# A long convolution beside attention on one core: two channels per matmul, filter rows in quarters

## The chip, the core and the metric

The kernel runs on one core of a Trainium2 chip. The metric is the device time of one execution in microseconds. Five engines work side by side: TensorE (PE, matmuls; PEld are its weight loads), VectorE (DVE), ScalarE (ACT), GpSimd (POOL) and SyncE (SP), which here only issues DMAs.

## The reference

Two independent blocks are computed and put side by side in the output (2048 x 1024, bf16).

- A: multi-head attention with S = 2048, D = 512 and 32 heads of 16: `qkv = x @ wqkv`, `p = softmax(q k^T / 4)`, `o = p v`, `out = o @ wo`.
- B: a gated long convolution of 512 channels. `k_shift` is `k` filtered along time with four taps per channel, `kv = k_shift * v`, then

```
y[t, c] = sum over u <= t of kv[u, c] * ssm_k[c, t - u]     (written as an FFT of length 4096)
y = y + kv * ssm_D
out = q * y
```

So for each channel B is a product with a lower triangular Toeplitz matrix of 2048 x 2048.

## The kernel before

**Attention.** Scores are made in blocks of 128 keys x 512 queries for one head; there are 2048 of them. A matmul (L728) puts a block in one of six PSUM banks. ScalarE takes the exp of two or three banks with one instruction (L761) into the ring PT. Part of the blocks, one in a step where VectorE has time, is done on VectorE with four operations: a scaling to fixed point (L803), two squaring steps (L810 twice) and a last step (L815), into the ring PTD. The PV matmuls (L844) accumulate in bank PVB. `finish_group` turns and normalises the result; `op_mm` multiplies with `wo`.

**Steps and the planner.** The program is written out ahead of time by a planner in Python. It keeps a modelled time for each engine (`pe.t`, `dve.t`, `done`), and in a loop over steps T it emits the score matmuls and the exp of step T, the PV of step T - 2, background work and filler matmuls (`emit_qk`, `pv_step`, `emit_bg`, `warm_up`). Each engine then runs its list in order, with semaphore waits. The planner's constants are PACE, RATE, CAP, LAGS (how many convolution lags a step may take), MARGIN, TURN, NEAR and HALF (by how much a background unit may overrun), PLAN (the step by which the work is spread), and FETCH (after how many us a block of 256 instructions of TensorE is counted as loaded; `Tensor.spare` holds work back near that point). Up to step N_OPEN the background units of the list `early` run, in bank BGB or PVB; after it those of `jobs`, for which a bank is taken from the steps for a few steps (a window, `win`, `hold`). A VectorE operation that frees a bank is placed at once (`urgent`); the rest of VectorE's work is put into the gaps (`advance`).

**The convolution.** The taps of `k_shift` are diagonal matrices (DG); `pe_unit` makes `k_shift` of 128 channels and 512 times in a bank, and `evac_unit` multiplies it with v into KV (L511 to L514). The filter, reversed in time and padded, is written to DRAM once (`kz_scratch`, from KZS). `load_wr` reads for each channel a [128, 2048] tile of it in which partition p starts one element after partition p - 1 (L996): 512 KB per channel, four channels (one `qd`) per slot of WR, four slots, the last of which is free only when the v tiles that it holds at first are used up. `conv_lags` makes for a `qd` 16 lags of 128 times, each as four matmuls, one per channel, in four groups of 32 columns of the array: the weights are KV (128 times x up to 16 blocks), the moving operand 128 columns of WR. Lag n pairs each block with the block n before it. Out come 16 of each 32 partitions of bank BGB. After four `qd` VectorE copies the bank to YB (L1028), and after eight `conv_turn` makes eight transposes of YB on TensorE and one multiplication with q (L1048). WR's DMAs all go through SP's queue, and a slot's reload is issued when the slot's last lag is done.

Of the kernel before, what the change touches and what calls it, by code (L numbers as in the profile page):

```python
# [9 lines left out]
U16 = mybir.dt.uint16  # L10

S = 2048
# [11 lines left out]
C = 512  # L24
NB = S // 128
PAD = 128
# [3 lines left out]
R_W = 16  # L30
# [6 lines left out]
N_OPEN = 66  # L37
# [26 lines left out]
CLOSE = 12  # L64
# [7 lines left out]
PLAN = 710  # L72
# [3 lines left out]
Q_DUE = 24  # L76
# [9 lines left out]
DMA_KB = 394  # L86
X_KB = 200
WINDOW = 3.4
HALF = 0.25
TURN = 0.2  # L90
SOON = 0.5
NEAR = 0.2
FULL = 1.6
BUSY = 0.85
FILL_GAP = 0.2
RATE = 4.2
CAP = 14.0
WAIT = 1.5
LATE = 0.2
# [8 lines left out]
FETCH = 6.3  # L108
# [111 lines left out]
def bass_concat_heads__mha_block__ssm_conv_h3__prompt_kernel(  # L220
# [36 lines left out]
    KV = sb("KV", [128, C // 4, NB, 4])  # L257
# [143 lines left out]
    h_va1 = pool.op(lambda e: e.memset(VA[:, :, :, 8 * VW:VROW].rearrange("p s k e -> p (s k) e"), 1.0))  # L401
    h_qt0 = pool.op(lambda e: e.memset(QT[:, 1:R_Q, :, :].rearrange("p r n f -> p (r n f)"), 0.0), us=(1.5, 1.6))
# [87 lines left out]
    def evac_unit(u, bank, h):  # L490
        kind = u[0]
        if kind == "q":
            p = u[1]
            last = [qk_done[2 * (p - R_Q) + i] for i in range(2)] if p >= R_Q else []
            hh = urgent(lambda e: e.tensor_scalar(QS[:, :], PS[:, bank, :], QSCALE, None, ALU.mult),
                        [h] + [h_q[2 * (p - 1) + i] if p > 1 else None for i in range(2)], us=V512)
            for par in range(2):
                for r0 in range(16 * par, 128, 32):
                    h_q[2 * p + par] = dma(pool, d_qs[p % 2][par], QT[r0:r0 + 16, p % R_Q, par, :], QS[r0:r0 + 16, :],
                                           [hh, h_qt0] + last, kb=16)  # L500
        elif kind == "k":
            _, o, sc = u
            c0 = KEYS0 if (o, sc) == (0, 0) else 0
            hh = urgent(lambda e: e.tensor_copy(KTo[:, o % 2, sc * 512 + c0:(sc + 1) * 512], PS[:, bank, c0:512]),
                        [h, qk_done[LAST[o - 2]] if o > 1 else None], us=(0.335, 0.46) if c0 else V512)
            h_k[(o, sc)] = hh
            if (o, sc) == (3, 3):
                load_wop(h)
        elif kind == "kv":
            _, c, i = u  # L510
            dst = KV[:, 32 * c:32 * c + 32, NB - 4 - 4 * i:NB - 4 * i, :]  # L511
            val = VST[c][:, NB - 4 - 4 * i:NB - 4 * i, :].rearrange("p b (k c) -> p k b c", c=4)
            src = PS[:, bank, :].rearrange("p (b k c) -> p k b c", b=4, c=4)
            h_kvc[c] = hh = urgent(lambda e: e.tensor_tensor(dst, src, val, ALU.mult), [h, h_vn[c]], us=V512)  # L514
            kv_n[c] += 1
            if sum(kv_n[0:2]) == 8 and c < 2:
                load_qn(0, [h])
                wr_free.append((R_W // 4 - 1, hh))
                load_wr()
            if c >= 2 and kv_n[c] == 4:  # L520
                h_kvm[c - 2] = h
        else:
            _, o, sc = u
            dst = VA[:, o % 2, 4 * sc:4 * sc + 4, 0:8 * VW].rearrange("p k (h e) -> p k h e", e=VW)[:, :, :, 0:DH]
            src = PS[:, bank, :].rearrange("p (k h e) -> p k h e", k=4, h=8)
            hh = urgent(lambda e: e.tensor_copy(dst, src), [h, h_va1, pv_last[LAST[o - 2]] if o > 1 else None], us=V512)
            h_v[(o, sc)] = hh
        bank_free[bank] = hh
# [456 lines left out]
    h_yb = [None]  # L985
# [4 lines left out]
    def load_wr():  # L990
        while wr_free and wr_next[0] < C // 4:
            (i, dep), qd = wr_free.pop(0), wr_next[0]
            wr_next[0] += 1
            wr_slot[qd] = i
            for c in range(4):
                src = bass.AP(tensor=kz_ap.tensor, offset=kz_ap[4 * qd + c, 0].offset, ap=[[1, 128], [1, S]])  # L996
                h_wr[qd] = dma(sp, d_wr[i], WR[:, 4 * i + c, :], src, [h_kzw[0], dep])
# [4 lines left out]

    def conv_lags(qd, n0, n1):
        kk = qd % 8
        deps = [h_wr[qd], h_kvc[qd // 32]]
        r = 4 * wr_slot[qd]
        if kk % 4 == 0 and n0 == 0:
            deps.append(bank_free[BGB])

        def fn(e):  # L1010
            ins = None
            for n in range(n0, n1):
                for c in range(4):
                    ins = e.matmul(PS[32 * c:32 * c + NB - n, BGB, 128 * (kk % 4):128 * (kk % 4) + 128],  # L1014
                                   lhsT=KV[:, qd, n:NB, c],
                                   rhs=WR[:, r + c, 128 * (NB - 1 - n):128 * (NB - n)],
                                   start=(n == 0), stop=(n == NB - 1), tile_position=(0, 32 * c))
            return ins
        h = pe.op(fn, deps, run=LAG * (n1 - n0), kind="C", lat=0.4)
        if n1 == NB:  # L1020
            wr_free.append((wr_slot[qd], h))
            load_wr()
            if kk % 4 == 3:
                half = kk // 4
                src = PS[:, BGB, :]
                src = bass.AP(tensor=src.tensor, offset=PS[:, BGB, 127:128].offset,
                              ap=[src.ap[0], [128, 4], [-1, 128]])
                hh = urgent(lambda e: e.tensor_copy(YB[:, half, :].rearrange("p (k i) -> p k i", k=4), src),  # L1028
                            [h, h_yb[0]], slack=S_C, us=V512)
                bank_free[BGB] = h_ybw[0] = hh  # L1030
        return h

    def conv_turn(b, bank):
        pbf = PS[:, bank, :].bitcast(BF16)

        def fn(e):
            ins = None
            for k in range(8):
                ins = e.transpose(pbf[:, 128 * k:128 * k + 128], YB[:, k // 4, 128 * (k % 4):128 * (k % 4) + 128],
                                  IDN[:, :])  # L1040
            return ins
        h = pe.op(fn, [bank_free[bank], h_ybw[0], h_idn], run=0.445, kind="F")
        h_yb[0] = h
        sl = b // 8
        yv = pbf.rearrange("p (c j) -> p c j", j=32)[:, :, 0:NB].rearrange("p c j -> p j c")
        yv = bass.AP(tensor=yv.tensor, offset=pbf[:, NB - 1:NB].offset, ap=[yv.ap[0], [-1, NB], [32, CHB]])
        qv = QN[:, :, CHB * (b % 8):CHB * (b % 8) + CHB]
        hh = urgent(lambda e: e.tensor_tensor(qv, yv, qv, ALU.mult), [h, h_qn[sl]], slack=S_C, us=V512)  # L1048
        bank_free[bank] = hh
        if b % 8 == 7:  # L1050
            dst = out2[:, D + 256 * sl:D + 256 * (sl + 1)].rearrange("(t p) c -> p t c", p=128)
            ho = dma(pool, d_outB[0], dst, QN[:, :, :], [hh], kb=1600)
            if sl == 0:
                load_qn(1, [ho])
# [4 lines left out]
    units = [("kv", c, i) for c in range(2) for i in range(4)] + [(x, 1, i) for i in range(4) for x in "kv"]  # L1059
# [7 lines left out]
    jobs += [(step(9 + 7 * c) - 8, ("kv", c + 2, i)) for c in range(2) for i in range(4)]  # L1067
    jobs += [(step(25 + 2 * qb) + 8 * t, ("op", qb, t)) for qb in range(NQB - 1) for t in range(4)]
    jobs.sort(key=lambda j: j[0])
    state = {"qd": 0, "lag": 0, "turn": False, "started": False, "lags": 0.0, "left": C // 4 * NB, "t": 0.0}  # L1070
# [6 lines left out]
    def next_unit(T):  # L1077
        if T < N_OPEN:
            return early[0] if early and ready(early[0][1]) else None
        if state["turn"]:  # L1080
            return T, ("turn", state["qd"] // 8 - 1)
        return next((j for j in jobs if ready(j[1])), None)
# [5 lines left out]
    def unit_step(T):  # L1088
# [7 lines left out]
        while not tight:  # L1096
# [23 lines left out]
            us = pe.turn("F") + (0.445 if u[0] == "turn" else 0.478 if u[0] in ("kv", "v") else 2 * MM) + SWITCH  # L1120
# [22 lines left out]
    def emit_bg(T):  # L1143
# [5 lines left out]
        if T - end[0] in tail_mm:  # L1149
            assert st["qd"] == C // 4 and not st["turn"], (T, st)  # L1150
# [3 lines left out]
        if st["qd"] == C // 4 and not st["turn"]:  # L1154
# [3 lines left out]
        if st["turn"] and st["qd"] == C // 4:  # L1158
# [11 lines left out]
        while left > 0 and st["qd"] < wr_next[0] and kv_n[st["qd"] // 32] == 4 and at(h_wr[st["qd"]]) + WAIT <= pe.t:  # L1170
            if st["turn"] and st["qd"] % 4 == 3 and st["lag"] + left >= NB:
                left = NB - 1 - st["lag"]
                if left <= 0:
                    break
# [3 lines left out]
            n1 = min(n0 + left, NB)  # L1178
# [4 lines left out]
            st["lag"] = n1 % NB  # L1183
            if n1 == NB:
                st["qd"] += 1
                if st["qd"] % 4 == 0:
                    st["turn"] = st["turn"] or st["qd"] % 8 == 0
                    break

    def filler_place(limit):  # L1190
# [5 lines left out]
        if state["started"] and state["lag"]:  # L1196
            return BGB, 0, NB, 128 * (state["qd"] % 4), 1, False
# [53 lines left out]
    assert state["qd"] == C // 4 and not state["turn"] and not jobs and not part[0], (state, jobs)  # L1251
# [65 lines left out]
```

## Time and profile before

| | |
|---|---|
| three runs | 825.12, 829.2, 827.42 us; median 827.42 us |
| the profiled execution | 828.52 us, of which the span from first to last instruction is 826.8 us |
| ScalarE, VectorE, TensorE busy | 807.0, 794.2, 762.2 us |
| DMA | 291.41 MB, 109,235 packets; q1 (SP's queue) busy for 90.8% |
| exp instructions on ScalarE (L761) | 722, for 1771 blocks |
| blocks on VectorE (L803) | 277 |
| WR<-kz_scratch | 512 DMAs of 512 KB, median 8.4 us from issue to landing |

The busy times of an engine come from its instructions as the profiler saw them, so instructions that overlap are counted once. In a group's line stand the line of the kernel, engine, operation, output <- input with shapes, the count, then the busy time and the mean length of one, then the idle time of the engine before them and what ended it. "issue" is time in which an engine waited for nothing that the profile shows. A DMA share above 1.00 in a short stretch comes from packets that overlap.

### The profile page before, as it was taken

The numbers are of one execution on the slowest core, as the hardware profiler recorded it, in microseconds if no ns is written. First come the engines' busy times: TensorE is split into PE (matmuls) and PEld (weight loads), VectorE is DVE, ScalarE is ACT, GpSimd is POOL, SyncE is SP. The second block draws the span as 40 slices with busy tenths as digits, with TensorE's granted clock in tenths as the row PEclk, the third lists the DMA queues.
The fourth block names the chain that finished last, engine by engine and source line by source line (L and its number), as shares of the span: only waits on it lengthen the run. The fifth ranks groups of instructions, "written<-read, shape, count | busy, mean of one in ns | idle before, by whom it ended". The sixth has DMA issues, their size and how long they took to land.

```text
span 826.8 us, 30549 instructions
## 1 busy us (share of the span) xinstructions
PE 762.2 (92%) x13603; PEld 324.2 (39%) x13642; DVE 794.2 (96%) x1360; ACT 807.0 (98%) x727; POOL 78.7 (10%) x155
## 2 busy tenths in 40 slices
PE   8998989999999899999899999999999999998987
PEld 3343434443333344444333344444433333333332
DVE  4999999999999899999999999999999999999985
ACT  6999999999999899999999999999999999999987
POOL 3300320010100101001011010101002002010000
PEclk9999999999999999999999999999999999999999
DMA  9998499999999999999999899999999999999922
GB/s 220 233 300 304 151 382 404 385 379 407 393 407 405 394 401 389 405 354 367 394 388 391 318 372 383 394 408 387 408 407 352 378 393 362 399 382 367 375 83 77
DMA packets 109235, 291.41 MB, mean 352 GB/s; under 512 B 37680, under 2 KB 41648, under 8 KB 108720
## 3 DMA queue, kind: packets, MB, share of 16 engines
q1 hardware_dynamic: 102256, 280.80, 90.8%
q0 software_dynamic: 5648, 8.27, 3.1%
q8 instruction: 108, 1.77, 0.9%
q10 hardware_dynamic: 1200, 0.39, 0.2%
q14 instruction: 23, 0.19, 0.1%
HBM read 276.83 MB, written 6.42 MB: 343 GB/s over the span
## 4 chain that ended last, share of the span: by engine, by line
ACT 77%; DVE 10%; PE 9%; issue 2%; DMA 1%; SPq 0%
ACT PT L761 77%; DVE EH L810 4%; PE PS L728 3%; DVE FX L803 2%; PE PS L1014 2%; PE PS L844 2%; DVE PTD L815 2%; PE PS L1219 1%; PE PS L468 1%; DMA xT<-in_A_x_dram 1%; DVE DT L905 0%; DVE YB L1028 0%; SPq L312 0%; DVE KV L514 0%; DVE OTN L925 0%
## 5 line engine op out<-in xcount | busy, mean ns | idle before, releaser
L761 ACT ACTIVATE PT<-PS 128x1024 bf16<-128x1024 f32 (+2 forms) x722 | 804.1, 1376 | 8.8 <-PE PS L728 8.3
L728 PE MATMUL PS<-QT,KTo 32*128 32x512 bf16 x2048 | 287.1, 385 | 38.7 <-ACT PT L761 14.1
L844 PE MATMUL PS<-PT,VA 128*32 128x512 bf16 x1771 | 199.7, 391 | 6.6 <-issue 3.5
L1014 PE MATMUL PS<-WR,KV 128*12 128x128 bf16 (+15 forms) x8192 | 201.6, 220 | 4.4 <-issue 4.3
L803 DVE TENSOR_SCALAR FX<-PS 128x512 f32<-128x512 f32 x277 | 187.9, 682 | 8.3 <-PE PS L728 8.0
L815 DVE SCALAR_TENSOR_TENSOR PTD<-EH,FX 128x512 uint16<-128x512 f32 x277 | 185.7, 677 | 0.0
L810 DVE SCALAR_TENSOR_TENSOR EH<-EH 128x512 f32<-128x512 f32 x277 | 185.4, 680 | 0.0
L810 DVE SCALAR_TENSOR_TENSOR EH<-FX 128x512 f32<-128x512 uint16 x277 | 184.5, 682 | 0.1
L1014 PEld LDWEIGHTS PS<-WR,KV 128*12 128x12 bf16 (+15 forms) x8192 | 140.6, 88 | 71.9 <-issue 42.5
L728 PEld LDWEIGHTS PS<-QT,KTo 32*128 32x128 bf16 x2048 | 73.3, 91 | 237.8 <-ACT PT L761 178.9
L1219 PE MATMUL PS<-IDN,ZW 128*32 128x512 bf16 (+3 forms) x498 | 132.2, 334 | 0.0
L312 POOL DMA_DIRECT2D QT<-QS x120 | 59.2, 501 | 483.7 <-DVE DR L912 133.7
L844 PEld LDWEIGHTS PS<-PT,VA 128*32 128x32 bf16 x1771 | 48.0, 93 | 114.0 <-issue 97.5
L844 PE MATMUL PS<-PTD,VA 128*32 128x512 bf16 x277 | 83.1, 383 | 0.0
L1219 PEld LDWEIGHTS PS<-IDN,ZW 128*32 128x32 bf16 x498 | 41.8, 96 | 24.1 <-issue 10.4
L905 DVE STREAM_TRANSPOSE DT<-PS 128x512 f32<-128x512 f32 x32 | 22.7, 709 | 7.3 <-PE PS L844 6.8
L1028 DVE CAST YB<-PS 128x512 bf16<-128x512 f32 x32 | 21.9, 684 | 1.4 <-PE PS L1219 1.1
L844 PEld LDWEIGHTS PS<-PTD,VA 128*32 128x32 bf16 x277 | 20.4, 95 | 1.6 <-DVE PTD L815 0.2
L955 PE MATMUL PS<-WKV,OTN 128*128 128x512 bf16 x53 | 16.9, 383 | 2.1 <-issue 1.6
L479 PE MATMUL PS<-WKV,xT 128*128 128x128 bf16 x256 | 18.1, 220 | 0.1
L456 PE MATMUL PS<-xT,WKV 128*128 128x512 bf16 (+1 forms) x52 | 15.0, 373 | 2.9 <-issue 1.1
L447 PE MATMUL PS<-xT,WQ 128*128 128x512 bf16 x45 | 14.4, 382 | 2.4 <-issue 2.1
(65 smaller groups left out, 209.2 us busy)
## 6 DMA issues: line engine op xcount, KB each, us to landing
WR<-kz_scratch SPq DMA_DIRECT2D x512, 512.0 KB, 8.4
kz_scratch<-WR SPq DMA_DIRECT2D x1, 2176.0 KB, 8.3
QN<-in_B_q_dram POOLq DMA_DIRECT2D x2, 1024.0 KB, 12.4
out_dram<-QN POOLq DMA_DIRECT2D x2, 1024.0 KB, 8.6
QT<-QS POOLq DMA_DIRECT2D x120, 16.0 KB, 5.3
out_dram<-OUTA POOLq DMA_DIRECT2D x12, 128.0 KB, 5.2
QN<-in_B_ssm_k_dram SPq DMA_DIRECT2D x1, 1024.0 KB, 8.3
OTN<-in_B_ssm_k_dram SPq DMA_DIRECT2D x1, 1024.0 KB, 9.2
```

The source lines that it names most:

```text
L312: f(outp, inp).then_inc(dsem.sem, 16)
L479: ins = e.matmul(PS[:, bank, 128 * j:128 * j + 128], lhsT=xT[:, dc, (4 * sc + j) * 128:(4 * sc + j + 1) * 128], rhs=WV[:, dc, o * 128:(o + ...
L728: ins = e.matmul(PS[:, bank, :], lhsT=KTo[32 * s:32 * s + 32, OF[n_] % 2, kt * 128:(kt + 1) * 128], rhs=QT[32 * s:32 * s + 32, n_ // 2 % R ...
L761: h_exp[T] = act.op(lambda e: e.activation(PT[:, p0:p0 + n, :].rearrange("p b f -> p (b f)"), PS[:, banks[0]:banks[0] + n, :].rearrange("p ...
L803: h_f = urgent(lambda e: e.tensor_scalar(fx, PS[:, bank, :], FIX_ADD, FIX_HI, ALU.add, ALU.min), [h, h_last.get(i - R_FX)], slack=S_FX)
L810: st["h"] = dve.op(lambda e: e.scalar_tensor_tensor(eh, src, (P1, P2)[j], src, ALU.add, ALU.mult), [st["h"], h_last.get(i - R_EH)], us=us)
L815: lambda e: e.scalar_tensor_tensor(out16, eh, P3, fx, ALU.mult, ALU.add),
L844: ins = e.matmul(dst, lhsT=w, rhs=rhs, start=(k == 0), stop=(k == KT - 1), tile_position=(0, 32 * s))
L905: h_t = urgent(lambda e: e.transpose(out=dt, in_=PS[:, PVB, :]), [h, h_mul.get(n - 1)], slack=S_T, us=(0.63, 0.751))
L1014: ins = e.matmul(PS[32 * c:32 * c + NB - n, BGB, 128 * (kk % 4):128 * (kk % 4) + 128], lhsT=KV[:, qd, n:NB, c], rhs=WR[:, r + c, 128 * (NB ...
L1028: hh = urgent(lambda e: e.tensor_copy(YB[:, half, :].rearrange("p (k i) -> p k i", k=4), src), [h, h_yb[0]], slack=S_C, us=V512)
L1219: pe.op(lambda e, s=s, k=k, rhs=rhs, bank=bank, rows=rows, c0=c0, first=first: e.matmul(PS[32 * s:32 * s + rows, bank, c0:c0 + 128 * k], l ...
```

## The change

A `qd` is now eight channels in place of four. The 128 rows of the array are split between two channels, 64 times each. The channel pair of a group is 64 channels apart.

- WR has 8 rows in place of 16: two slots. A row holds two channels, 64 partitions each, so a `qd` still has four rows. Its filter tile comes in eight DMAs: four quarters of 512 columns, the last columns first, and for each quarter the two halves of 64 partitions in turn, four rows per DMA (256 KB).
- KV is twice as large and mostly zero for the other channel: a column has the values of one channel in its 64 partitions and zeros in the others, which GpSimd writes once at the start. `evac_unit` therefore splits each product into four operations of 64 partitions.
- `conv_lags` makes 32 lags of 64 times for a `qd`, in the order 0, -1, 1, 2, ... 30, again as four matmuls each; the weights have up to 32 columns (two channels x 16 blocks). Out come all 32 partitions of a group.
- A full bank now holds 32 channels, so VectorE copies half as many banks to YB, and a turn follows each of them, with four transposes.
- The kv units of the second 128 channels move from `early` to `jobs`, and constants of the planner are set anew.

```diff
+NLAG = S // 64
-R_W = 16
+R_W = 8
-N_OPEN = 66
+N_OPEN = 64
+KV1 = 2
-CLOSE = 12
+CLOSE = 10
-PLAN = 710
+PLAN = 715
-Q_DUE = 24
+Q_DUE = 28
+HALF_KB = 270
+WR_C = 512
-TURN = 0.2
+TURN = 0.05
-NEAR = 0.2
+NEAR = 0.1
-FILL_GAP = 0.2
+FILL_GAP = 0.25
-CAP = 14.0
+CAP = 18.0
-LATE = 0.2
+LATE = 0.1
-FETCH = 6.3
+FETCH = 4.2
...
-    KV = sb("KV", [128, C // 4, NB, 4])
+    KV = sb("KV", [128, C // 8, 2, 2 * NB, 4])
...
+    h_kv0 = pool.op(lambda e: e.memset(KV[:, :, :, :, :].rearrange("p o r u g -> p (o r u g)").bitcast(U32), 0), us=(8.8, 8.9))
     h_qt0 = pool.op(lambda e: e.memset(QT[:, 1:R_Q, :, :].rearrange("p r n f -> p (r n f)"), 0.0), us=(1.5, 1.6))
...
-            dst = KV[:, 32 * c:32 * c + 32, NB - 4 - 4 * i:NB - 4 * i, :]
-            val = VST[c][:, NB - 4 - 4 * i:NB - 4 * i, :].rearrange("p b (k c) -> p k b c", c=4)
-            src = PS[:, bank, :].rearrange("p (b k c) -> p k b c", b=4, c=4)
-            h_kvc[c] = hh = urgent(lambda e: e.tensor_tensor(dst, src, val, ALU.mult), [h, h_vn[c]], us=V512)
+            q0 = 2 * (NB - 4 - 4 * i)
+            val = VST[c][:, NB - 4 - 4 * i:NB - 4 * i, :].rearrange("p b (h o g) -> p b h o g", h=2, g=4)
+            src = PS[:, bank, :].rearrange("p (b h o g) -> p b h o g", b=4, h=2, g=4)
+            for half in range(2):
+                for ch in range(2):
+                    hs, cs = slice(64 * half, 64 * half + 64), slice(64 * ch, 64 * ch + 64)
+                    dst = KV[cs, 16 * c:16 * c + 16, 1 - half, q0 + ch:q0 + 8:2, :].rearrange("p o q g -> p q o g")
+                    h_kvc[c] = hh = (dve.op if half or ch else urgent)(
+                        lambda e, dst=dst, hs=hs, ch=ch: e.tensor_tensor(dst, src[hs, :, ch], val[hs, :, ch], ALU.mult),
+                        [h, h_vn[c], h_kv0], us=(0.335, 0.46))
...
-            for c in range(4):
-                src = bass.AP(tensor=kz_ap.tensor, offset=kz_ap[4 * qd + c, 0].offset, ap=[[1, 128], [1, S]])
-                h_wr[qd] = dma(sp, d_wr[i], WR[:, 4 * i + c, :], src, [h_kzw[0], dep])
+            for c0 in range(S - WR_C, -1, -WR_C):
+                for ch in range(2):
+                    row = 128 * (qd // 16) + 64 * ch + 4 * (qd % 16)
+                    src = bass.AP(tensor=kz_ap.tensor, offset=kz_ap[row, c0].offset, ap=[[1, 64], [LKZ, 4], [1, WR_C]])
+                    h_wr[qd] = dma(sp, d_wr[i], WR[64 * ch:64 * ch + 64, 4 * i:4 * i + 4, c0:c0 + WR_C], src,
+                                   [h_kzw[0], dep], kb=WR_C // 2, rate=HALF_KB)
...
+    DIST = [0, -1] + list(range(1, NLAG - 1))
...
-                for c in range(4):
-                    ins = e.matmul(PS[32 * c:32 * c + NB - n, BGB, 128 * (kk % 4):128 * (kk % 4) + 128],
-                                   lhsT=KV[:, qd, n:NB, c],
-                                   rhs=WR[:, r + c, 128 * (NB - 1 - n):128 * (NB - n)],
-                                   start=(n == 0), stop=(n == NB - 1), tile_position=(0, 32 * c))
+                d = DIST[n]
+                w = 64 if d < 0 else 128
+                for g in range(4):
+                    kv = KV[:, qd, (1 + d) % 2, (1 + d) // 2 * 2:2 * NB, g]
+                    ins = e.matmul(PS[32 * g:32 * g + 2 * ((30 - d) // 2 + 1), BGB, 128 * kk:128 * kk + w],
+                                   lhsT=kv, rhs=WR[:, r + g, S - 64 * d - 128:S - 64 * d - 128 + w],
+                                   start=(n == 0), stop=(n == NLAG - 1), tile_position=(0, 32 * g))
...
-            for k in range(8):
-                ins = e.transpose(pbf[:, 128 * k:128 * k + 128], YB[:, k // 4, 128 * (k % 4):128 * (k % 4) + 128],
-                                  IDN[:, :])
+            for k in range(4):
+                ins = e.transpose(pbf[:, 128 * k:128 * k + 128], YB[:, b % 2, 128 * k:128 * k + 128], IDN[:, :])
...
-    units = [("kv", c, i) for c in range(2) for i in range(4)] + [(x, 1, i) for i in range(4) for x in "kv"]
+    units = [("kv", 0, i) for i in range(4)] + [(x, 1, i) for i in range(4) for x in "kv"]
...
+    jobs += [(N_OPEN + KV1 + 4 * i, ("kv", 1, i)) for i in range(4)]
...
-                    st["turn"] = st["turn"] or st["qd"] % 8 == 0
+                    st["turn"] = True
```

## The prediction

> **What bounds the kernel now.** I read the page from the busy shares to the DMA queues and the chain, then the groups of instructions with their shapes kept apart, then the busy time by stretch, and last the timeline around the stretches where ScalarE lost time. First the page: busy shares, then two DMA queues, then the chain that ended last.
>
> ```profile
> PE 762.2 (92%) x13603; PEld 324.2 (39%) x13642; DVE 794.2 (96%) x1360; ACT 807.0 (98%) x727; POOL 78.7 (10%) x155
> q1 hardware_dynamic: 102256, 280.80, 90.8%
> q8 instruction: 108, 1.77, 0.9%
> ACT 77%; DVE 10%; PE 9%; issue 2%; DMA 1%; SPq 0%
> ```
>
> ScalarE is busy for 98% of the span and 77% of the chain is its exp; VectorE stands at 96%; the DMA engines at 91%. All three look full, but only the first sets the end: ScalarE has 1771 of the 2048 score blocks, VectorE 277. The groups (line, engine, shape, count, busy us, mean ns):
>
> ```profile
> L761 ACT ACTIVATE PT<-PS 128x1536 bf16<-128x1536 f32 x321 | 493.9, 1605 | 6.5 <-PE PS L728 6.0
> L761 ACT ACTIVATE PT<-PS 128x1024 bf16<-128x1024 f32 x398 | 429.0, 1188 | 1.0 <-PE PS L728 1.0
> L1028 DVE CAST YB<-PS 128x512 bf16<-128x512 f32 x32 | 21.9, 684 | 1.4 <-PE PS L1219 1.1 <-PE PS L1014 0.2
> L916 DVE TENSOR_TENSOR DTN<-DT,DR 128x256 bf16<-128x256 f32 x32 | 13.3, 415 | 0.0
> ```
>
> The means overlap their neighbours. Taken from start to next start, the usual step is 1.330 us for three blocks and 0.903 us for two, so one block costs ScalarE 0.427 us and one more instruction 0.05 us. On VectorE a 512-column operation takes 0.600 us and a 256-column one 0.332 us in the same way, so a block there costs 4 x 0.600 = 2.4 us. With 321, 398 and 3 instructions (of three, two and four blocks) the floor of ScalarE's exp is 792 us; the trace has 804 busy, so about 12 us are short waits inside the busy time.
>
> Now the stretches (length, then busy time of PE, PEld, DVE, ACT, POOL, clock, DMA share, GB/s):
>
> ```profile
> 80.00:100.00 20.00, 19.29 (x291) 7.54 (x290) 20.00 (x36) 20.00 (x20) 3.83 (x8) 1.00 0.33 99
> 240.00:320.00 80.00, 74.22 (x1455) 31.85 (x1459) 77.52 (x135) 77.93 (x71) 5.78 (x13) 0.98 1.03 400
> 480.00:560.00 80.00, 75.15 (x1484) 33.22 (x1475) 79.60 (x137) 80.00 (x74) 4.65 (x9) 1.00 1.02 396
> 784.00:788.00 4.00, 3.08 (x67) 1.11 (x55) 4.00 (x8) 4.00 (x5) 0.00 (x0) 1.00 1.03 405
> ```
>
> From 400 to 780 us ScalarE loses 0.1 us, with the DMA engines full. What it loses lies elsewhere, in six places, and they look alike. The last, from the timeline:
>
> ```profile
> 786.86 0.40 PE L844 MATMUL PS<-PT,VA 128*32 128x512 bf16 x3
> 789.23 0.40 PE L844 MATMUL PS<-PT,VA 128*32 128x512 bf16 x3 [1.98 <-issue]
> 790.87 2.85 ACT L761 ACTIVATE PT<-PS 128x1536 bf16<-128x1536 f32 x2 [2.13 <-PE PS L728]
> ```
>
> TensorE stops with nothing to wait for, and ScalarE runs dry behind it. In the packet records a 16 KB packet of the instruction queue ends 1.3 to 1.6 us before TensorE resumes, at all six (106.1, 223.8, 230.0, 279.9, 356.0, 789.2 us): TensorE waits for its own code. ScalarE loses 0.42 + 0.46 + 0.62 + 2.00 + 0.58 + 2.13 = 6.2 us there (at 280 and 788 the granted clock drops too), VectorE 7.9 us.
>
> **The change, part by part.**
>
> *Filter loads.* Before: 512 DMAs of 512 KB, 65,536 packets of 4 KB, median 159 ns. After: 64 rounds of 8 DMAs, still 512 issues on SP, each 256 KB, in 131,072 packets of 1 KB. Such packets are in the trace for other transfers: 46 ns median, 53 mean, 48 in the last stores. So 131,072 x 48 / 16 = 393 us of all engines against 65,536 x 170 (mean) / 16 = 696: q1 falls from 91% to about 54%. A round is 128 packets per engine, 6.1 us, plus about 2 us (the last stores land in 2.2 us): 8 us. Bounds: 46 ns, and 96 if 64 partitions take only half the rate; I take 48, from the same packet size. Nothing of this is on the path while loads land in time.
>
> *Ring.* WR has two slots in place of four, each a round of eight channels; a slot refills when its last lag is done. A round of 32 lags must last some 11 us (64 rounds in about 735 us), and one slot is consumed while the other fills. The planner books 8 x 256/270 + 4.2 = 11.8 us for a load and adds 1.5; against 8 us that is cover of 5 us. The second slot is only free when the kv units of c = 1 are done, about 16 steps after N_OPEN: the first rounds run from one slot, which costs pace, not time.
>
> *Code loads.* With fewer queued packets ahead of them the 108 code packets arrive sooner, and the planner's FETCH goes from 6.3 to 4.2. Gain between 0 and 6.2 us. For it: the worst stall, from 787 us, begins at a DMA share of 1.03, and where the share is 0.33 (80 to 100 us) ScalarE loses nothing. Against: from 400 to 780 us the share is as high and nothing is lost either, so the load alone does not make a stall. I take 60%: -3.7 us. VectorE gets 0.6 x 7.9 = 4.7 us back, two blocks, 2 x 0.427 = -0.85 us.
>
> *Convolution matmuls.* 128 x 16 x 4 = 8192 before, 64 x 32 x 4 = 8192 after; 128 columns again (64 for one lag in 32). A group of four starts every 56 ns, the same for 16 weight columns as for one. After, up to 32 columns are loaded. No row has four 32-column loads per 56 ns; the nearest in the timeline:
>
> ```profile
> 500.50 0.10 PEld L844 LDWEIGHTS PS<-PT,VA 128*32 128x32 bf16 x4 [0.23 <-issue]
> 503.25 1.07 PE L479 MATMUL PS<-WKV,xT 128*128 128x128 bf16 x16
> ```
>
> L479's matmuls, each with a load of 128 columns, take 1.07/16 = 64 to 67 ns. Four loads of 16 columns fit into 56 ns; if they only just fit and follow one another, four of 32 take 112 ns, the other end. Against that, the four loads of the PV group above, 32 columns each and 93 ns long by the mean, lie within 0.10 us, so they start within 10 ns of each other. I take 56 ns, hence 0; at 64 ns it is 2048 x 8 = 16 us over 645 steps, 25 ns a step, beside 179 us in which TensorE waits for ScalarE. The other end is a rival below. [...]
>
> *VectorE.* YB evacuations fall from 32 to 16: -16 x 0.600 = -9.6 us. Each of 16 kv evacuations becomes four of 64 x 256: 16 x (4 x 0.332 - 0.600) = +11.6. No row has 64 partitions; at most each costs the full 0.600 (+28.8). Net +2.0 us (up to +19), 0.85 block, +0.36 us on ScalarE (up to +3.4).
>
> *TensorE units and steps.* Turns shrink from eight transposes to four, and the allowed overruns TURN and NEAR from 0.20 to 0.05 and 0.10. Out of 12 us of short waits, 16 turns x 0.15 = 2.4 us at most; I take -1.5 (bounds -3 to +3). Four kv units move from the opening to windows behind N_OPEN: perhaps five more steps, 5 x 0.05 = +0.25.
>
> *GpSimd.* The KV memset (8192 words; L402 took 1.79 us for 2048 elements, so 7 us, at most 14) is queued before the QT and KZS memsets, make_dg, the K paddings and Q's DMAs. First needed at 39.8 us (kz_store) and 43.5 us (first kv product): hidden; uncovered it costs 7 us once.
>
> Sum: -3.7 - 0.85 + 0.36 - 1.5 + 0.25 = -5.4 us. The profiled execution took 828.5 us, span 826.8 and 1.7 around it, giving 823.1; it lies 1.1 us above the median of three, so I forecast 827.4 - 5.4 = 822.0.
>
> **The rivals.**
>
> *Nothing measurable.* The code stalls stay, or go elsewhere, since ScalarE's floor does not move: 827.4 + 0.6 = 828, between 823.3 and 831.6 with the bounds above. For it: 400 to 780 us already runs without loss under full DMA load.
>
> *The ring runs dry (slower).* If a half of 64 partitions is written at half the rate, a round takes 128 x 96 = 12.3 + 2 = 14.3 us, 1.0 us past what the planner books. The first lag of a round then waits on TensorE, and the QK and PV matmuls queued behind it with it. With 0.35 us of margin that is 0.65 us on ScalarE; in a third of 64 rounds 14 us (841), in all of them 42 us (869). It decides from about 88 ns a packet, (13.3 - 2)/128. Against: 46 to 53 ns in the records. A milder form, single late rounds, gives 832 to 836.
>
> *Weight loads bind (slower).* At 112 ns a group, 2048 x 56 = 115 us more on TensorE; of these 0.18 us a step most falls in time in which it waits for ScalarE (179 us in all); a third on the path gives 866. It decides once a step's waits are used up, from about 0.28 us a step. Against: the overlap above.
>
> **How the numbers follow.** 0.5%, 4.1 us, is about what a measurement of this kernel can tell. Forecast case 0.50 (faster than 823.3; 817 to 823), no measurable change 0.27, dry ring 0.18, weight loads 0.05. The low end, 817, takes all 6.2 us, all 7.9 us of VectorE (1.4) and 3 us of short waits, less 0.6; the high end, 835, takes in the mild dry ring and leaves out about 0.14 above and 0.06 below.
>
> **What would show it.** Right: q1 at 50 to 60%, fewer issue waits on TensorE above 0.6 us, ScalarE idle before L761 below 4 us, 276 to 280 blocks on VectorE, 56 ns groups. Wrong: L1014 waiting for WR's DMA (dry ring); lag groups far above 56 ns; L514 near 0.6 us each; more than 740 exp instructions; stalls of the same size at other times.

## The result, and the profile after

The changed kernel takes 881.19 us (median of four runs, 876.27 to 886.56), beside 828.31 us (825.12 to 831.45) for the kernel before: 1.064 times as long, interval 1.056 to 1.072. The forecast was 822.0 us, with a range up to 835. It was wrong in sign.

The profiled execution took 886.56 us, its span 884.8. From the page of the changed kernel: busy shares, two DMA queues, and the chain that ended last.

```profile
PE 787.4 (89%) x13569; PEld 329.5 (37%) x13569; DVE 805.2 (91%) x1388; ACT 815.3 (92%) x732; POOL 85.5 (10%) x156
q1 hardware_dynamic: 167792, 146.58, 76.2%
q8 instruction: 107, 1.75, 0.9%
ACT 46%; PE 23%; DVE 17%; DMA 6%; issue 5%; SPq 3%; POOL 0%; DVEq 0%
```

Every share but GpSimd's has gone down; no engine has become the bound. ScalarE's part of the chain falls from 77% to 46%, TensorE's rises from 9% to 23%. Of the 58.0 us by which the span grew, ScalarE was idle for 49.7 (884.8 - 815.3 = 69.5 against 826.8 - 807.0 = 19.8) and busy for 8.3. And q1 is still busy for 76%, though its bytes fell from 280.80 to 146.58 MB. The groups of instructions, with shapes kept apart:

```profile
L773 ACT ACTIVATE PT<-PS 128x1536 bf16<-128x1536 f32 x312 | 464.9, 1537 | 24.3 <-PE PS L740 23.9
L773 ACT ACTIVATE PT<-PS 128x1024 bf16<-128x1024 f32 x412 | 427.0, 1114 | 33.0 <-PE PS L740 32.7
L1047 DVE CAST YB<-PS 128x512 bf16<-128x512 f32 x16 | 11.0, 686 | 7.2 <-PE PS L1034 6.0 <-PE PS L1237 1.0
L525 DVE TENSOR_TENSOR KV<-PS,WR 64x256 bf16<-64x256 f32 x32 | 13.4, 420 | 0.8
```

The exp is done by 727 instructions (312, 412 and 3) in place of 722, and a single one takes no more time than before (1537 and 1114 ns, 1605 and 1188 before). What is new stands behind the bars: 24 and 33 us in which ScalarE waited for the score matmuls (L740), in place of 6.5 and 1.0. What TensorE waited for, from the list of waits of the changed kernel (total us, times, longest):

```profile
ACT PT L773 <- PE PS L740: 57.6, 76, 2.8
...
PE PS L1034 <- issue: 27.3, 16, 3.1
...
PEld PS L1034 <- DMA WR<-kz_scratch: 7.9, 11, 1.7
...
PE PS L1034 <- DMA WR<-kz_scratch: 4.2, 5, 1.6
```

The convolution matmuls (L1034) waited for their filter tiles only 11 times, 7.9 us together: the list has these waits at the weight loads (PEld), and five of them, 4.2 us, once more at the matmul behind the load. But they stopped 16 times with nothing to wait for, up to 3.1 us. Before, the same line of the list reads:

```profile
PE PS L1014 <- issue: 4.3, 7, 1.2
```

One such stop in the timeline of the changed kernel (start, length, engine, ..., idle time before):

```profile
189.63 0.34 PE L1034 MATMUL PS<-WR,KV 128*4 128x128 bf16 x11
...
193.07 0.37 PE L1034 MATMUL PS<-WR,KV 128*2 128x128 bf16 x5 [3.10 <-issue]
...
194.03 1.02 ACT L773 ACTIVATE PT<-PS 128x1024 bf16<-128x1024 f32 x1 [2.78 <-PE PS L740]
```

It is the picture that the prediction read at 789 us of the kernel before: TensorE stops inside a row of matmuls, and ScalarE runs dry behind it. In the packet records a 16 KB packet of the instruction queue q8 ends 1.0 to 1.9 us before TensorE resumes. Stops of this kind over 0.8 us number 5 before (7.0 us together) and 21 after (36.5 us). (The expectations below, written on a first count, say 22.) At 4 of the 5 and 14 of the 21 (27.6 us) the profile names nothing else that TensorE waited for, and these lie a multiple of 256 instructions apart, to within one, in TensorE's list: the size of a block of code. At the others it also names another engine or a filter tile. What can follow a stop is seen in the busy time by stretch around this one (length; busy time of PE, PEld, DVE, ACT, POOL; clock, DMA share, GB/s):

```profile
190.00:194.00 4.00, 0.93 (x12) 0.28 (x13) 1.39 (x3) 1.25 (x1) 0.00 (x0) 0.78 0.73 158
194.00:200.00 6.00, 6.00 (x60) 1.89 (x60) 4.37 (x8) 4.49 (x4) 0.00 (x0) 0.58 0.83 189
...
480.00:560.00 80.00, 71.81 (x1194) 29.64 (x1182) 74.96 (x127) 75.04 (x71) 9.77 (x19) 0.98 0.79 185
```

The clock record has TensorE at half the clock from 192.2 us, inside the stop, to 199.0 us. Behind the stop it is busy throughout (6.00 of 6 us) and ScalarE only for 4.49. So such a stop is paid for twice: once as the stop, once as the slow stretch behind it. Not every stop is: a half-clock stretch of 3.4 to 10.2 us begins in, or within 2 us behind, 13 of the 21 (before: 2 of the 5). Within the span the clock records show 78.5 us at half clock in the changed kernel, in 15 stretches, and 6.8 in 2 before. ScalarE is idle for 45.9 us between the start of a stop and 1.2 us behind it or at half clock, and for 5.6 before: that is 40 of the 49.7 us. And the stops now lie in the middle too: from 480 to 560 us ScalarE is busy for 75.04 us, where it had 80.00 before.

The filter tiles themselves, from the packet records: a 1 KB packet of WR's loads takes 75 ns in the mean, that is 300 ns for 4 KB, against 169.5 ns for a 4 KB packet before. A round of eight channels takes 10.4 us. The kernel before needed 2 x 5.76 = 11.5 us for the same eight channels, with twice the bytes. Halving the bytes bought almost nothing, since they move at half the rate: 185 GB/s in the stretch above, 396 in the same stretch before.

### The profile page after: what moved, and what is told of

It is laid out like the page before. It is cut to its first block, busy times and chain, and to the rows that moved or that the text cites. A ratio compares the mean times of both kernels' runs of the same rounds, so it can differ in the third digit from the quotient of the medians.

```text
span 884.8 us, 30455 instructions
## 1 busy us (share of the span) xinstructions
PE 787.4 (89%) x13569; PEld 329.5 (37%) x13569; DVE 805.2 (91%) x1388; ACT 815.3 (92%) x732; POOL 85.5 (10%) x156
## 3 DMA queue, kind: packets, MB, share of 16 engines
q1 hardware_dynamic: 167792, 146.58, 76.2%
## 4 chain that ended last, share of the span: by engine, by line
ACT 46%; PE 23%; DVE 17%; DMA 6%; issue 5%; SPq 3%; POOL 0%; DVEq 0%
ACT PT L773 45%; PE PS L740 8%; DVE EH L822 6%; PE PS L1034 5%; PE PS L856 5%; DMA WR<-kz_scratch 4%; DVE FX L815 4%; DVE PTD L827 3%; DVE KV L525 3%; SPq L317 3%; PE PS L1237 2%; DMA QT<-QS 1%; PE PS L462 1%; DVE DT L917 1%; PE PS L967 1%
## 5 line engine op out<-in xcount | busy, mean ns | idle before, releaser
L773 ACT ACTIVATE PT<-PS 128x1536 bf16<-128x1536 f32 (+2 forms) x727 | 812.4, 1299 | 58.5 <-PE PS L740 57.6
L740 PE MATMUL PS<-QT,KTo 32*128 32x512 bf16 x2048 | 297.5, 397 | 43.5 <-ACT PT L773 11.1
L1034 PE MATMUL PS<-WR,KV 128*30 128x128 bf16 (+8 forms) x8192 | 201.8, 224 | 31.7 <-issue 27.3
L856 PE MATMUL PS<-PT,VA 128*32 128x512 bf16 x1772 | 204.5, 402 | 8.3 <-DVE DT L917 5.2
L1034 PEld LDWEIGHTS PS<-WR,KV 128*32 128x32 bf16 (+7 forms) x8192 | 145.8, 96 | 99.4 <-issue 67.1
L740 PEld LDWEIGHTS PS<-QT,KTo 32*128 32x128 bf16 x2048 | 73.1, 91 | 233.0 <-ACT PT L773 149.6
L1237 PE MATMUL PS<-IDN,ZW 128*32 128x512 bf16 (+3 forms) x487 | 125.7, 333 | 0.2 <-DVE DT L917 0.2
L967 PE MATMUL PS<-WKV,OTN 128*128 128x512 bf16 x64 | 20.1, 394 | 0.3 <-DVE OTN L937 0.3
L462 PE MATMUL PS<-xT,WKV 128*128 128x512 bf16 (+1 forms) x64 | 18.8, 399 | 1.3 <-DVE KV L525 0.6
L453 PE MATMUL PS<-xT,WQ 128*128 128x512 bf16 x60 | 18.5, 400 | 0.1
L510 DVE CAST KTo<-PS 128x512 bf16<-128x512 f32 (+1 forms) x16 | 10.7, 670 | 7.7 <-PE PS L462 7.7
## 6 DMA issues: line engine op xcount, KB each, us to landing
QN<-in_B_q_dram POOLq DMA_DIRECT2D x2, 1024.0 KB, 10.5
```

The costliest lines, as they stand in the source:

```text
L462: return e.matmul(PS[:, bank, c0:512], lhsT=WK[:, dc, o * 128:(o + 1) * 128], rhs=xT[:, dc, sc * 512 + c0:(sc + 1) * 512], start=(dc == 0) ...
L740: ins = e.matmul(PS[:, bank, :], lhsT=KTo[32 * s:32 * s + 32, OF[n_] % 2, kt * 128:(kt + 1) * 128], rhs=QT[32 * s:32 * s + 32, n_ // 2 % R ...
L773: h_exp[T] = act.op(lambda e: e.activation(PT[:, p0:p0 + n, :].rearrange("p b f -> p (b f)"), PS[:, banks[0]:banks[0] + n, :].rearrange("p ...
L856: ins = e.matmul(dst, lhsT=w, rhs=rhs, start=(k == 0), stop=(k == KT - 1), tile_position=(0, 32 * s))
L967: ins = e.matmul(PS[:, bank, :], lhsT=OTN[:, PAIRS.index((o, qb)), t * 128:(t + 1) * 128], rhs=WO[:, o, :], start=(o == 0), stop=(o == 3))
L1034: ins = e.matmul(PS[32 * g:32 * g + 2 * ((30 - d) // 2 + 1), BGB, 128 * kk:128 * kk + w], lhsT=kv, rhs=WR[:, r + g, S - 64 * d - 128:S - 6 ...
```

## The experiments

Three questions were open. Do the filter loads cause the stops, or does the new order of the program? If the loads do, through which path: late tiles, the planner's FETCH, or code packets held back? And what makes the loads slow: the packet size, the half tiles, or the order of the halves? "Stops" below are TensorE's code stops of over 0.8 us in the profiled execution, and "ns per 4 KB" the mean time of WR's packets, 1 KB packets times four.

**e1: the kernel before with the new booking of code loads.**

```diff
-FETCH = 6.3
+FETCH = 4.2
```

> The kernel before with one constant changed: FETCH 4.2 in place of 6.3, so that its planner counts TensorE's code as loaded 2.1 us earlier, as the changed kernel does. Loads and convolution stay as they were. Theory A (the planner's shorter FETCH is what brought the code stalls): stalls of TensorE of over 0.8 us behind a code packet rise from 5 towards the 22 of the changed kernel, and the time from 828 to 850 to 880 us. Theory B (the filter traffic of the changed kernel itself delays the code, or the rounds come too late): at most a few more stalls, 828 to 838 us.

Measured: 826.91 us beside 827.23, ratio 0.998 (0.995 to 1.002); 3 stops. Booking code loads as landed sooner costs the kernel before nothing. FETCH alone is not the cause.

**e2: whole rows, in place of quarters.**

```diff
-WR_C = 512
+WR_C = 2048
```

> The changed kernel with WR_C 2048 in place of 512: a round is two DMAs of 64 partitions x four rows x 4 KB, the same bytes in packets of 4 KB. If the size of the packets sets the rate (1 KB at 75 ns where 48 was expected): 160 to 170 ns a packet, a round in 5.5 to 6 us in place of 10.4, time 830 to 860 us, fewer code stalls. If the half of the partitions sets it: about 300 ns a packet, a round in 10 us as before, time 870 to 890 us.

Measured: 979.65 us, ratio 1.180 (1.170 to 1.191). Packets are 4 KB again and take 305 ns, against 169 in the kernel before. So the packet size is not what makes the loads slow. What is left is the tile of 64 partitions, or the four rows in one DMA; e8 and e10, with one row per DMA, speak for the tile (254 ns in e8's first `qd` of halves, 295 in e10). With the eight quarters gone, a round is two DMAs of 1 MB, one for each half. The waits of this run:

```profile
ACT PT L773 <- PE PS L740: 146.7, 123, 5.5
...
PE PS L1034 <- issue: 70.6, 23, 5.4
```

At nearly the same rate per byte as in the changed kernel there are 36 stops, of up to 5.4 us, and 195 us at half clock. That one packet now takes 305 ns and not 75 is one reading, and the order of the halves (e10) another.

**e3 and e4: three slots; the old FETCH too.**

```diff
-R_W = 8
+R_W = 12
```

and for e4 also

```diff
-FETCH = 4.2
+FETCH = 6.3
```

> The changed kernel with R_W 12 in place of 8: three slots in the ring of filter tiles. If late rounds of filter tiles cost the time (ring runs dry): the waits of L1034 for WR (12 us) go, time 850 to 865 us. If the code stalls cost it: 875 to 890 us, with about 20 of them left, since FETCH is still 4.2.

> The changed kernel with three slots (R_W 12) and FETCH back at 6.3. Theory A: code stalls of over 0.8 us fall from 22 to under 8, the half-clock time from 80 us to under 20 us, time 825 to 845 us. Theory B: the stalls stay above 12 and the time above 860 us, since the traffic is the same.

Measured: 880.05 us (1.060, 1.048 to 1.073) and 877.49 us (1.057, 1.045 to 1.070), with 19 and 17 stops. Neither is told apart from the changed kernel. With a third slot no wait for a filter tile is left in either list, and there were only 7.9 us of waiting for them; so the dry ring is not where the time goes.

**e5 and e6: the two halves on two queues.** The upper half's loads go through GpSimd's queue, with semaphores of their own; e6 also has `WR_C = 2048`. Theory P of the expectations from here on is an assumption of the author's: the loads are slow while one half of the partitions is written, and the code is late with them.

```diff
+    d_wp = [DmaSem(sem(f"d_wp{i}")) for i in range(R_W // 4)]
...
-                    h_wr[qd] = dma(sp, d_wr[i], WR[64 * ch:64 * ch + 64, 4 * i:4 * i + 4, c0:c0 + WR_C], src,
+                    h_wr[qd][ch] = dma((sp, pool)[ch], (d_wr, d_wp)[ch][i], WR[64 * ch:64 * ch + 64, 4 * i:4 * i + 4, c0:c0 + WR_C], src,
...
```

> The changed kernel, with the upper half of the partitions (64 to 127) loaded through GpSimd's queue and the lower half through SP's, so that both halves are in flight together; the same bytes, the same 1 KB packets, the same plan. [...] Rival Q (the rate comes from the form of the reads, four rows per partition or overlapping reads of DRAM): packets stay at 75 ns, 20 or more stalls, 870 to 890 us.

> The same with WR_C 2048, packets of 4 KB, one DMA for each half of a round. Theory P: about 170 to 200 ns a packet in place of 305, a round in 6 to 7 us, 825 to 850 us. Rival Q: 300 ns, 950 us or more, as with 2048 columns on one queue (980 us).

Measured: 924.81 us (1.117, 1.098 to 1.136) and 939.0 us (1.134, 1.120 to 1.149), 32 and 30 stops. SP's 1 KB packets still take 77 ns in e5, and GpSimd's queue carries its half in packets of 4 KB, at some 264 ns; in e6 4 KB take 268 ns on SP's queue and 273 on GpSimd's. Offering both halves at once doesn't bring the rate back. e6 beats e2 (939 against 980), in which the halves came one after the other; that mixing them is worth something is one reading of it, since half of the loads also changed queue. e5 is worse than the change itself.

**e7: a quarter of the traffic, the same program.** After a slot's first use each DMA loads one of its four rows.

```diff
+            rows = 1 if i in wr_slot.values() else 4
...
-                    src = bass.AP(tensor=kz_ap.tensor, offset=kz_ap[row, c0].offset, ap=[[1, 64], [LKZ, 4], [1, WR_C]])
-                    h_wr[qd] = dma(sp, d_wr[i], WR[64 * ch:64 * ch + 64, 4 * i:4 * i + 4, c0:c0 + WR_C], src,
+                    src = bass.AP(tensor=kz_ap.tensor, offset=kz_ap[row, c0].offset, ap=[[1, 64], [LKZ, rows], [1, WR_C]])
+                    h_wr[qd] = dma(sp, d_wr[i], WR[64 * ch:64 * ch + 64, 4 * i:4 * i + rows, c0:c0 + WR_C], src,
```

> The changed kernel, where after the first use of a slot each DMA loads one row of its four, so that the filter traffic is a quarter and the plan, the matmuls and the number of DMAs are the same; three of four filter rows are those of an earlier round. Theory B/P (the traffic delays the code and sets the clock back): stalls of over 0.8 us under 6, half-clock time under 15 us, 818 to 828 us. If the schedule itself is what is slow (wider weights, four kv operations, two slots): 850 us or more.

Measured: 832.44 us beside 828.53, ratio 1.0063 (1.0033 to 1.0094), with 2 stops (2.3 us) and 12.3 us at half clock. At both of the stops (65 and 112 us) the profile names VectorE, and the changed kernel has them too; a stop with nothing else to wait for is not left. This is the experiment that decides: the plan, the instructions and their order are the same, and with three quarters of the filter bytes gone 49 of the 53 us are gone. The waits of e7, and its busy time from 480 to 640 us (columns as above):

```profile
ACT PT L773 <- PE PS L740: 10.0, 20, 1.3
```

```profile
480.00:640.00 160.00, 149.01 (x2843) 64.17 (x2851) 159.29 (x272) 159.96 (x145) 16.14 (x33) 1.00 0.22 57
```

ScalarE is full again, as it was before. About 4 us stay, and they lie early. First the kernel before, then e7:

```profile
40.00:80.00 40.00, 36.94 (x402) 17.43 (x404) 40.00 (x68) 39.68 (x34) 1.21 (x1) 1.00 0.98 327
80.00:160.00 80.00, 74.99 (x1394) 33.54 (x1394) 78.93 (x136) 79.45 (x74) 11.46 (x24) 1.00 0.85 314
```

```profile
40.00:80.00 40.00, 33.66 (x332) 13.55 (x332) 38.41 (x70) 36.83 (x31) 0.00 (x0) 0.96 0.59 141
80.00:160.00 80.00, 71.01 (x1066) 29.71 (x1063) 77.18 (x138) 76.62 (x73) 12.72 (x25) 0.98 0.31 72
```

From 40 to 160 us e7 loses (39.68 + 79.45) - (36.83 + 76.62) = 5.7 us of ScalarE against the kernel before; this is the stretch with the kv units, now four VectorE operations each, and the start of the ring. From 160 to 820 us it gains 4.0 us (657.1 busy against 653.1). So the gain that the prediction hoped for, from code that lands sooner, exists. It takes a quarter of this change's traffic to get it, and the opening takes it back.

**e8: half tiles in a part of the kernel before.** The tiles of `qd` 40 to 59 come in two DMAs of 64 partitions, one 4 KB row each; all else is the kernel before.

```diff
-                src = bass.AP(tensor=kz_ap.tensor, offset=kz_ap[4 * qd + c, 0].offset, ap=[[1, 128], [1, S]])
-                h_wr[qd] = dma(sp, d_wr[i], WR[:, 4 * i + c, :], src, [h_kzw[0], dep])
+                n = 64 if 40 <= qd < 60 else 128
+                for p0 in range(0, 128, n):
+                    src = bass.AP(tensor=kz_ap.tensor, offset=kz_ap[4 * qd + c, p0].offset, ap=[[1, n], [1, S]])
+                    h_wr[qd] = dma(sp, d_wr[i], WR[p0:p0 + n, 4 * i + c, :], src, [h_kzw[0], dep], kb=4 * n)
```

> The kernel before, with each filter tile of rounds 40 to 59 loaded by two DMAs of 64 partitions, one row each, in place of one DMA of 128; bytes and 4 KB packets as before. Theory P: in this stretch, and in no other, packets take about 300 ns in place of 169. Rival Q: 160 to 180 ns throughout.

Measured: 851.22 us (one run) beside 828.53, 9 stops. Its busy time ahead of the stretch with half tiles, at its beginning, and later in it:

```profile
240.00:280.00 40.00, 35.95 (x719) 15.26 (x722) 39.81 (x70) 39.76 (x36) 3.81 (x8) 1.00 1.02 394
...
292.00:300.00 8.00, 5.72 (x110) 2.38 (x107) 5.80 (x12) 5.60 (x5) 0.00 (x0) 0.84 1.03 262
...
340.00:400.00 60.00, 52.31 (x1021) 24.27 (x1021) 52.63 (x89) 55.37 (x52) 0.00 (x0) 1.00 1.03 353
```

The same bytes to the same addresses: as soon as they come in halves the rate falls from 394 to 262 GB/s at a full DMA share, and ScalarE and TensorE lose time. A packet takes 163 ns in most `qd` outside the stretch (in the mean of a `qd`), 254 in its first `qd`, then 234, 227, 219, 217, 213, and 184 to 198 from the seventh to the nineteenth. The last takes 228, and so does `qd` 60, which comes whole again; then it is 163. In a stream that never pauses, halves in turn recover most of the rate within some 45 us, and for the next 70.

**e9 and e10: the order of the halves.** Both load one whole row (4 KB) per partition and 64 partitions per DMA, eight DMAs a round; e9 takes lower and upper half in turn, e10 four lower, then four upper.

```diff
-            for c0 in range(S - WR_C, -1, -WR_C):
-                for ch in range(2):
...
+            for g, ch in [(g, ch) for g in range(4) for ch in range(2)]:
+                row = 128 * (qd // 16) + 64 * ch + 4 * (qd % 16) + g
+                src = bass.AP(tensor=kz_ap.tensor, offset=kz_ap[row, 0].offset, ap=[[1, 64], [1, S]])
+                h_wr[qd] = dma(sp, d_wr[i], WR[64 * ch:64 * ch + 64, 4 * i + g, :], src,
+                               [h_kzw[0], dep], kb=256, rate=HALF_KB)
```

and for e10

```diff
-            for g, ch in [(g, ch) for g in range(4) for ch in range(2)]:
+            for g, ch in [(g, ch) for ch in range(2) for g in range(4)]:
```

> The changed kernel, its rounds cut another way: eight DMAs of 256 KB as before, but each is one row of 64 partitions x 4 KB, lower and upper half in turn (before: four rows x 1 KB). Bytes, plan and number of DMAs are the same. Theory P in its narrower form (the rate falls because most engines write the same half at one time; four packets of an engine before the half changes let them mix): 190 to 220 ns a packet as in the stretch of halves in the kernel before, a round in 6.5 to 7.5 us, code stalls of over 0.8 us down from 22 to 8 to 14, 840 to 860 us. Rival Q (any tile of 64 partitions is slow by its reads): about 300 ns, 870 to 980 us.

> The same eight DMAs of one row each as in the run with rows in turn, only ordered: the four rows of the lower half first, then the four of the upper. If writing one half at a time is what halves the rate: about 300 ns a packet, a round in 10 to 11 us, 40 code stalls, 930 to 980 us, as with two DMAs of four rows of 2048 columns. If the form of the DMA (four rows, packets) is what counts: as with rows in turn.

Measured: e9 862.58 us (1.040, 1.030 to 1.050), 268 ns, 16 stops; e10 897.41 us (1.082, 1.070 to 1.094), 295 ns, 23 stops. The waits of e9:

```profile
ACT PT L773 <- PE PS L740: 34.8, 50, 3.0
...
PE PS L1033 <- issue: 21.3, 17, 3.1
```

and of e10:

```profile
ACT PT L773 <- PE PS L740: 68.9, 80, 4.6
...
PE PS L1033 <- issue: 33.2, 18, 4.9
```

The two differ in the order of eight DMAs and in nothing else, and lie 35 us apart. Byte for byte the same loads stop TensorE for longer when one half is loaded for 5 us on end (33.2 us of such waits against 21.3).

**e11: e9 with three slots and the old FETCH.** 

> Rows in turn, with three slots and FETCH 6.3. A round in 6.5 to 7.5 us leaves the engines idle for a third of the time; with the code booked at what it takes under load (5.9 us by the packet records of the kernel before): 3 to 8 code stalls, 826 to 840 us. If the bursts alone make the stalls: 8 or more stalls and 840 to 860 us.

Measured: 870.45 us (1.050, 1.029 to 1.070), 269 ns, 15 stops; not told apart from e9. Here too neither the ring nor FETCH matters.

**e12: engines set out of step.** e9, and ahead of each round a DMA of 8 partitions. The author's assumption, which no trace here shows, is that it makes a few engines start later, so that lower and upper half are written at the same time.

```diff
+    SC = sb("SC", [128, 4, S])
...
+            src = bass.AP(tensor=kz_ap.tensor, offset=kz_ap[4 * qd, 0].offset, ap=[[1, 8], [LKZ, 4], [1, S]])
+            last, h_pre[0] = h_pre[0], d_pre.add()
+            sp.op(lambda e, src=src: e.dma_start(SC[0:8, :, :], src).then_inc(d_pre.sem, 16), [h_kzw[0], dep, last], inc=False, us=(0.0, 0.0))
...
```

> Rows in turn, and ahead of each round one more DMA: 8 partitions x four rows x 4 KB into a spare tile that nobody reads (128 KB, 6% more bytes). By its 8 partitions it is expected to occupy eight of the 16 engines for as long as one row DMA occupies each, so that from then on eight engines write the lower half while the other eight write the upper. [...] Theory R (the two channels that a round reads lie 278 KB apart in DRAM, and that costs the rate): 268 ns, 860 to 870 us.

Measured: 932.04 us (1.127, 1.119 to 1.136), 309 ns, 24 stops. It made the loads slower. Either the added DMA doesn't spread the engines as assumed, or their being in step is not the reason; this experiment doesn't say which.

**e13: both halves from the same channel.** e9, but the upper half reads the lower half's channel, 64 elements on, as the kernel before does.

```diff
-                row = 128 * (qd // 16) + 64 * ch + 4 * (qd % 16) + g
-                src = bass.AP(tensor=kz_ap.tensor, offset=kz_ap[row, 0].offset, ap=[[1, 64], [1, S]])
+                row = 128 * (qd // 16) + 4 * (qd % 16) + g
+                src = bass.AP(tensor=kz_ap.tensor, offset=kz_ap[row, 64 * ch].offset, ap=[[1, 64], [1, S]])
```

> Rows in turn, but both halves of the partitions read the same channel, the upper half 64 elements further on, as the tiles of the kernel before do; the filters of half of the channels are thus not read. Theory R (where the rows lie in DRAM): about 200 ns a packet, a round in 6.5 to 7.5 us, 835 to 850 us. Theory P (the halves of SBUF): 268 ns and 9.9 us as with rows in turn, 858 to 868 us.

Measured: 864.99 us (1.046, 1.043 to 1.050), 269 ns, 15 stops, as e9. That the two halves read different channels, far apart in DRAM, is not what slows the loads.

Side by side, six of the kernels with one queue:

| WR's loads | ns per 4 KB | stops | at half clock, us | time, us |
|---|---|---|---|---|
| before: 128 partitions | 169 | 5 | 7 | 828 |
| a quarter of the change's traffic (e7) | 261 | 2 | 12 | 832 |
| rows, halves in turn (e9) | 268 | 16 | 34 | 863 |
| the change: quarters in turn | 300 | 21 | 79 | 881 |
| rows, half by half (e10) | 295 | 23 | 85 | 897 |
| 1 MB per half (e2) | 305 | 36 | 195 | 980 |

In this table, with the traffic in full, the time rises with the stops, and the stops are most where one half is loaded longest on end. That is not the whole account: e5 and e6 have 32 and 30 stops though both halves are offered at once, and e12 has 24. None of the thirteen kernels is faster than the kernel before; e1 is level with it.

## Why the prediction was wrong, point by point

**Filter loads: the step that failed first.** The 48 ns came from 1 KB packets of other transfers; the row that matched in size did not match in where the packets go. Measured: 75 ns, so WR's loads take 131,072 x 75 / 16 = 614 us of all engines and not 393, q1 stands at 76% and not 54%, and a round takes 10.4 us and not 8. The upper bound, 96 ns "if 64 partitions take only half the rate", was the one to weigh: at 4 KB e2 has 305 ns against 169, 1.8 times, and e8 has 254 against 163 in its first `qd` of halves, in the kernel before. Why 64 partitions are slower is not shown. How much it helps to load the halves in turn, the runs say: in e9's rounds little (268 ns), in e8's long stream most of it (184 to 198). And in e7, with a quarter of the traffic, the median 1 KB packet takes 46 ns (mean 65): the 48 ns are met when the traffic is thin, and not in a full stream.

**"Nothing of this is on the path while loads land in time": the path that was overlooked.** The loads did land in time, but for 7.9 us. The kernel lost through the code, which queue q8 loads beside them: 21 stops, and 2 with a quarter of the filter traffic (e7).

**Code loads: a wrong bound, and the step that decided the sign.** The prediction bounded this term between 0 and 6.2 us of gain and excluded a loss, arguing that there would be fewer packets ahead of the code. It reasoned with the share of busy time. But 188 GB/s at a share of 0.86 (100 to 850 us) go with 21 stops, where 385 GB/s at 1.01 (before, 100 to 780 us) go with 5. Code packets took 1226 ns in the mean, against 1055 before. The stops show at which instruction TensorE needs each packet. From the time at which it stood 256 instructions ahead of that one to the landing of the packet it is 2.8, 4.3, 5.8 and 7.3 us before (10th, 50th and 90th percentile, and the longest), 2.0, 4.2, 6.1 and 8.5 after, and 1.7, 4.6, 7.6 and 10.5 in e2. (The 5.9 us in e11's expectation were counted from an earlier point.) From before to after the median does not move; the late ones get later, and the late ones make the stops. In e7 it is 1.3, 1.9, 2.8 and 5.9 us, though a code packet itself takes 1053 ns, as before: what the filter traffic lengthens is mainly the time ahead of the packet. So the gain that the prediction argued for is real, but it comes with thinner traffic, and this change did not make it thin. The prediction held the warning itself: it had seen that a full load alone does not make a stop, so the share of busy time could not be what decides, and it had no row with half tiles beside code packets. A term without a near row needs a bound on both sides of nothing.

What holds a code packet back inside a DMA engine is not shown.

**The dry ring, the rival on the right side,** named the half rate as its source, and for it 841 to 869 us. Its mechanism did not decide: WR was waited for 11 times, for 7.9 us (e3, with a third slot and no such wait, is no faster). So its price came near for the wrong reason, and the range, which held only its mild form, missed.

**VectorE: mis-sized.** A 64 x 256 operation takes 0.453 us from start to next start, not 0.332. The kv evacuations cost 16 x (4 x 0.453 - 0.600) = 19.4 us and not 11.6; with the 9.6 us saved on YB (16 copies, as predicted) the net is +9.8 us and not +2.0, some 4 blocks or 1.7 us on ScalarE. It was inside the bounds given. Of its 64 operations 40 lie in the stretch from 40 to 160 us in which e7 loses its 5.7 us; how much of that is this term was not separated.

**What held.** Groups of four lag matmuls still start every 56 ns, also with 18 to 28 weight columns (mean 58 to 63), so the weight loads do not bind. Exp instructions rose by five, to 727. VectorE has 276 blocks, one fewer. GpSimd's memset took 6.9 us from 3.1 us on, and the first kv product came at 43.0 us against 43.5 before. And the reading of the bound held, in a way that should have warned: with ScalarE at 98%, a change that relieves the DMA engines had at most the 6 us of stops to win.

## What to carry to other kernels

Take a price per packet from packets that go to the same number of partitions in as full a stream. Here 48 ns became 75, and halving the bytes by halving the partitions left the DMA time nearly where it was (10.4 us for eight channels against 11.5). Before relieving an engine that does not bound the kernel, list all that share it, the instruction stream too, and give each a loss as well as a gain. And a stop of TensorE can cost more than its length: 13 of the 21 here had 3.4 us or more at half clock with them. So count the stops, not the share.

## What the runs showed of the hardware that was not expected

- The order of the halves matters, and whether they read one channel or two does not: 295 ns per 4 KB half by half, 268 in turn (e10, e9), 269 in turn from one channel (e13).
- In an unbroken stream, halves in turn speed up from 254 to 184–198 ns in some 45 us, and the last tile takes 228 again (e8). Why is not shown. The changed kernel, at 300 ns per 4 KB, pauses between its rounds (median 0.7 us); e12, which was to set the engines out of step, gave 309 ns.
- Half as many bytes per us can hold up TensorE's code more than twice as many: 21 stops at 188 GB/s in the changed kernel, 5 at 385 in the kernel before.
- A quarter of the filter traffic brings the code in 1.9 us (median) where the changed kernel has 4.2 and the kernel before 4.3, although the code packet itself takes no less time than before (1053 and 1055 ns) (e7).
